# Tile-wise waits for re-opened pools, bank pairs in order of completion, and weights fetched two ahead in a three-part transformer kernel

## Chip, cores and metric

The kernel runs on one core of a Trainium2 chip. The metric is the device time of one execution in microseconds, as the median of several runs; before the change it is 1088.41 us.

## What is computed

```python
def reference(**kwargs):
    attn_out = _attn_ref(**attn_kwargs)     # 4 batches, 12 heads, 448 tokens, head size 64
    B, H, S, D = attn_out.shape
    x = np.ascontiguousarray(attn_out.transpose(0, 2, 1, 3)).reshape(B * S, H * D)   # 1792 x 768
    x = _moe_ref(x=x, **moe_kwargs)
    return _moe2_ref(x=x, **moe2_kwargs)

def _attn_ref(q, k, v, cap):
    scores = scale * np.matmul(q, k.transpose(0, 1, 3, 2))
    scores = cap * np.tanh(scores / cap)
...
def _moe_ref(x, w_in, w_out):
    h = x @ w_in                            # 768 -> 2048
    g = h - np.tanh(h)
    return (g @ w_out).astype(np.float32)   # 2048 -> 768

def _moe2_ref(x, w_in, w_out):
    h = x @ w_in
    g = h * (1.0 / (1.0 + np.exp(-1.702 * h)))
    return (g @ w_out).astype(np.float32)
```

The two weight pairs arrive as float64; activations are float32.

## The kernel before

Every large product is done with three matmuls on fp32r operands: an operand is split into a high part (`hi_act`, a cast on ScalarE, L75) and a low part (`lo_dve`, a subtraction on VectorE, L87), and high x high, low x high and high x low are summed in PSUM. The float64 weights are read as pairs of 32-bit words and turned to float32 on chip (L192 on ScalarE, L201 and L207 on VectorE), then split into `wh` and `wl`, of which three buffers each exist.

The 1792 tokens go through in two parts: part 0 of 768 tokens, whose first up projection is partly run inside attention, and part 1 of 1024. A part is worked in two halves called spans, of 384 or 512 columns. The stages on the matmul engine (PE), with the time at which the profiled execution does them:

- 0 to 300 us: attention, and `gemm_in(0)` of part 0 (L848);
- 300 to 402 us: `gemm_out` (L878), the first down projection of part 0. It makes six 128-row outputs `e` in two "halves" of three. A half runs over eight weight chunks `j`; in each chunk the three sums of span 0 are added to, then the three of span 1, six matmuls each. After the last chunk `x_out` casts each finished sum on ScalarE and makes its low part on VectorE: these are the next layer's `x`;
- 402 to 504 us: `gemm_in(1)`, its result through a sigmoid GELU (L785);
- 504 to 592 us: `gemm_rows_seven` (L1073), the second down projection with seven block products (`ps_o`) in place of eight; its results leave through copies at L1109;
- 592 to 724 us: `gemm_in(0)` of part 1, its result through `g_cubic` (L749 on ScalarE, L750 on VectorE, then four more steps); 16 blocks `f`;
- 724 to 843 us `gemm_out_seven` (L920), to 960 us `gemm_in_seven` (L1002), to the end `gemm_rows_seven` again.

PSUM has eight banks. Two belong to `ps_s` for the whole program. The other six are used either as three pairs (pool `pair`) or as six single banks (pool `m`): `open_banks` closes one pool and opens the other on the same banks between stages. Likewise `swap_pools`, `open_plain` and `end_of_x` open SBUF pools in mid-program on bytes that released pools held. A pool opened in this way makes each of its new tiles wait for all users of the pools that held its bytes, whichever tile those used.

ScalarE, VectorE and the DMA queue of SyncE (SP) each work through their instructions in program order. A scheduler fixes that order from priorities; `tc.high_priority(offset=150)` moves what stands under it earlier.

Weights that are already float32 come as a stream: `w_next` hands out chunk `i`, `prepare` splits it, `fetch` starts the transfer from DRAM. Raw chunks land in the two buffers of `wr_p` (shown as `whole`); in `gemm_rows_seven` a third buffer, `spare`, is used for every third one. The chunks named `kept` are already split and land in `wh` and `wl` directly.

Of the kernel before, what the change touches and what calls it, by code (L numbers as in the profile page):

```python
# [9 lines left out]
F32 = mybir.dt.float32  # L10
# [24 lines left out]
def attention_moe_moe(ctx, tc, q, k, v, cap, w_in1, w_out1, w_in2, w_out2, out):  # L35
# [3 lines left out]
    P = 128  # L39
# [6 lines left out]
    KF = DF // P  # L46
# [11 lines left out]
    def pool(name, bufs, **kw):  # L58
        return ctx.enter_context(tc.tile_pool(name=name, bufs=bufs, **kw))
# [7 lines left out]
    ps_s = pool("ps_s", 2, space=bass.MemoryType.PSUM)  # L67
# [6 lines left out]
    def hi_act(dst, src):  # L74
        pin(nc.scalar.copy(out=dst, in_=src))  # L75
# [10 lines left out]
    def lo_dve(dst, src, hi):  # L86
        pin(nc.vector.tensor_tensor(out=dst, in0=src, in1=hi.bitcast(F32), op=ALU.subtract))  # L87
# [14 lines left out]
    xh, xl = list(xs_h[0]), list(xs_l[0])  # L102
# [25 lines left out]
    end_of_x = ExitStack()  # L128
# [5 lines left out]
    def open_second_x():  # L134
        some.pop("stack").close()
        end_of_x.close()
        n = TOKENS[1]
        rest = 2 * KM * (n - TOKENS[0])
        p = end_of_x.enter_context(tc.tile_pool(name="end_of_x", bufs=1, side="right"))
        t = p.tile([P, rest], F32R, name="x_end")  # L140
        slots = [x_big[:, a:a + n] for a in range(0, x_big.shape[1], n)] + [t[:, a:a + n] for a in range(0, rest, n)]
        xs_h.append(slots[:KM])
        xs_l.append(slots[KM:])
        open_temps()
# [20 lines left out]
    dbls, raws, whl, some = {}, {}, {}, {}  # L165
    n_raw, third = [0], []
# [110 lines left out]
    def fetch(i):  # L277
        if R0 <= i < len(stream) and not 0 <= i - R0 - len(rows_stream) < A0 and i not in whole:
            src, n, _ = stream[i]
            parts = src if isinstance(src, list) else [src]  # L280
            n_raw[0] += 1
            whole[i] = third[0] if third and n_raw[0] % 3 == 0 else wr_p.tile([P, WC], F32, tag="wr", name="whole")
            whole[i] = whole[i][:, :n]
            w = n // len(parts)
            for m, part in enumerate(parts):
                nc.sync.dma_start(out=whole[i][:, m * w:(m + 1) * w], in_=part)

    def prepare(upto):
        while n_ready[0] <= min(upto, len(stream) - 1):
            i = n_ready[0]  # L290
            if i < R0 and i not in early:
                with ExitStack() as behind:
                    if i < 2 * LEAD + 2:
                        for ins in marks:
                            behind.enter_context(tc.issue_after(ins))
                    convert(i)
                if i == R0 - 1:
                    fetch(R0)
                continue
            whl[i] = tuple(wh_p.tile([P, WC], F32R, tag=tag, name=tag) for tag in ("wh", "wl"))  # L300
            src, n, _ = stream[i]
            fetch(i)
            if i in whole:
                x = whole.pop(i)
                h, l = (t[:, :n] for t in whl[i])
                with tc.high_priority(offset=150):
                    hi_act(h, x)
                    lo_dve(l, x, h)
            else:
                for m, t in enumerate(whl[i]):  # L310
                    nc.sync.dma_start(out=t[:, :n].bitcast(F32), in_=src[:, m])
            fetch(i + 1)
            n_ready[0] += 1

    def w_next():
# [368 lines left out]
    def swap_pools(**kinds):  # L684
        if "stack" in some:
            some.pop("stack").close()
        some.clear()
        some["stack"] = ExitStack()
        for name, bufs in kinds.items():
            some[name] = some["stack"].enter_context(tc.tile_pool(name=f"some_{name}", bufs=bufs, side="right"))  # L690

    def open_wide():
        swap_pools(far=1, v=1)
# [7 lines left out]
    def open_banks(pairs):  # L701
        ps_stack.close()
        psum.clear()
        name, bufs = ("pair", 3) if pairs else ("m", 6)
        psum[name] = ps_stack.enter_context(tc.tile_pool(name=f"ps_{name}", bufs=bufs, space=bass.MemoryType.PSUM))
        if not pairs:
            for _ in range(2):
                one_bank("pass_over")

    def pair_of_banks(name):  # L710
        return psum["pair"].tile([P, 2, 512], F32, tag="pair", name=name)

    def one_bank(name):
        return psum["m"].tile([P, 512], F32, tag="m", name=name)
# [77 lines left out]

    def open_plain():
        g_stack.close()
        p = pool("g_plain", 1)
        gr.extend(p.tile([P, NT], F32, name=f"gr{i}") for i in range(KF))
        spare.append(p.tile([P, WC], F32, name="spare"))
        ring.extend([p.tile([P, HT], F32R, name=f"r{m}{i}") for m in "hl"] for i in range(KH))
# [32 lines left out]
    def gemm_in(layer):  # L831
        for f in f_order[layer]:
            i, (wh, wl) = w_next()
            pair = [] if "pair" not in psum else pair_of_banks("ps_h")
            for span, (a0, a1) in enumerate(SPANS[now[0]]):
                a = slice(a0, a1)
                if isinstance(pair, list):
                    pair.append(ps_s.tile([P, 512], F32, tag="s", name="ps_h")[:, :a1 - a0])
                    ps = pair[-1]
                else:  # L840
                    ps = pair[:, span, :a1 - a0]
                if layer:
                    seq = [(w, x, kk) for w, x in ((wh, xh), (wl, xh), (wh, xl)) for kk in range(KM)]
                else:
                    seq = [p for kk in range(KM) for p in ((wh, xh, kk), (wh, xl, kk))]
                    seq += [(wl, xh, kk) for kk in range(KM)]
                for m, (w, x, kk) in enumerate(seq):
                    pin(nc.tensor.matmul(ps, w[:, kk, :], x[kk][:, a], start=(m == 0), stop=(m == len(seq) - 1)))  # L848
                    if m == 0:
                        (beside_it if a0 else ahead)(i)  # L850
                    if m == LATE_AT:
                        run_late()
                    if m < len(seq) - 1:
                        yield
                if a0:
                    (g_cubic, g_gate)[layer](f, pair)
                yield

    def x_out(e, a, x):
        hi_act(xh[e][:, a], x)  # L860
        lo_dve(xl[e][:, a], x, xh[e][:, a])

    def gemm_out():
        for half in range(2):
            tiles = [pair_of_banks("ps_y") for _ in range(2 + half)]
            ps = [[t[:, span] for t in tiles] for span in range(2)]
            if not half:
                for bank in ps:
                    bank.append(ps_s.tile([P, 512], F32, tag="s", name="ps_y"))
            for j in range(KF // 2):  # L870
                i, (wh, wl) = w_next()
                for (a0, a1), bank in zip(SPANS[0], ps):
                    for e in range(3):
                        c = slice(e * P, (e + 1) * P)
                        seq = [p for kk in range(2) for p in ((wh, gh, kk), (wh, gl, kk))]
                        seq += [(wl, gh, kk) for kk in range(2)]
                        for m, (w, x, kk) in enumerate(seq):
                            nc.tensor.matmul(  # L878
                                bank[e][:, :a1 - a0], w[:, kk, c], x[2 * j + kk][:, a0:a1],
                                start=(j == 0 and m == 0), stop=(j == KF // 2 - 1 and m == len(seq) - 1),  # L880
                            )
                        if e == 0 and j < KF // 2 - 1:
                            (beside_it if a0 else ahead)(i)
                        if a0 == 0 and e == 1:
                            run_late()
                            if half == j == 0:
                                swap_pools(wd=1, wr=1)
                                dbl_dma()
                    if j == KF // 2 - 1:
                        for e in range(3):  # L890
                            x_out(3 * half + e, slice(a0, a1), bank[e][:, :a1 - a0])
                if j == KF // 2 - 1:
                    ahead(i)

# [138 lines left out]
    def gemm_rows_seven():  # L1033
# [10 lines left out]
            open_second_x()  # L1044
        room = [t[:, a:a + HW] for t in four_of_pairs() for a in (0, HW)]
        p1, u2 = room[:nt], room[nt:2 * nt]
        third.append(spare[0])
        todo = [divmod(n, KM) for n in range(2 * KM)] if another else []
        loaded = []
        step = 0  # L1050
# [2 lines left out]
        for p, name in enumerate(SEVEN_B):  # L1053
# [36 lines left out]
            for n in range(nt):  # L1090
# [9 lines left out]
                    rows_out(1, n, ps[n], u2[n])  # L1100
                elif not end:
                    rows_out(0, nt + n, ps[n])
        third.clear()

    def rows_out(half, n, ps, plus=None, two=False):
        tag = ("q", "v", "t", "far")[n % 4] if now[0] else ("q", "v", "q")[n % 3]
# [117 lines left out]
```

## Time and profile before

| | us |
|---|---|
| runs | 1084.84, 1088.41, 1088.77 |
| median | 1088.41 |
| the profiled execution, its own time | 1082.34 |
| its span in the trace | 1080.5 |
| PE busy in the span | 1065.3 (99%) |
| VectorE (DVE) busy | 806.2 (75%) |
| ScalarE (ACT) busy | 640.9 (59%) |

The span is what the trace covers, from the first instruction to the last; the profiled execution's own time is 1.84 us more. "Busy" of PE counts matmuls as the profile models them: a matmul's modelled end lies later than the start of the next, so a busy PE has no gap, but can still be slow if its clock is granted only in part (PEclk).

### The profile page before, as it was taken

The page shows a single profiled execution, that of the slowest core. Times are in us where ns is not written, and L with a number is a line of the kernel's source. Part 1 is how long each engine was busy: PE and PEld are TensorE (multiplying, and loading weights), DVE is VectorE, ACT ScalarE, POOL GpSimd, SP SyncE. Part 2 cuts the span into 40 slices and gives each one's busy share as a digit, 9 for nine tenths or more (in the row PEclk, how much of TensorE's full clock was granted, in tenths as well). Part 3 has the DMA queues.
Part 4 walks back from the last instruction along what each step waited for, and adds up shares of the span by engine and source line. Part 5 has one row for each costly group of instructions (what it writes and reads, how often), then busy time and mean ns, then how long its engine had stood idle before and what let it go on. Part 6 is the DMA issues. An engine that isn't in the chain of part 4 may idle for free.

```text
span 1080.5 us, 15254 instructions
## 1 busy us (share of the span) xinstructions
PE 1065.3 (99%) x5555; PEld 873.3 (81%) x5555; DVE 806.2 (75%) x1062; ACT 640.9 (59%) x850; POOL 54.5 (5%) x56
## 2 busy tenths in 40 slices
PE   9999999999999999999999999999999999999998
PEld 3333333799998999999999888878888788899998
DVE  4678989799986668676984688787968755489562
ACT  6898898699854344444673555564545443355552
POOL 0012343200000000000000000000000000000000
PEclk9999999999999999999999999999999999999999
DMA  6776678699769989886667885312332233334342
GB/s 143 184 215 197 183 198 252 201 311 300 252 216 365 346 288 358 307 296 194 199 203 227 298 283 176 107 48 75 101 102 82 94 91 98 93 100 129 98 126 73
DMA packets 146979, 205.58 MB, mean 190 GB/s; under 512 B 57628, under 2 KB 97112, under 8 KB 146904
## 3 DMA queue, kind: packets, MB, share of 16 engines
q1 hardware_dynamic: 145480, 203.82, 59.7%
q8 instruction: 44, 0.72, 0.3%
q10 hardware_dynamic: 1424, 0.79, 0.2%
q14 instruction: 31, 0.25, 0.1%
HBM read 145.49 MB, written 59.07 MB: 189 GB/s over the span
## 4 chain that ended last, share of the span: by engine, by line
PE 85%; DVE 5%; DMA 4%; ACT 3%; issue 2%; SPq 0%; DVEq 0%; ACTq 0%
PE ps_h L848 23%; PE ps_o L1073 19%; PE ps_y L920 11%; PE ps_h L1002 10%; PE ps_pv L530 7%; PE ps_sc L489 5%; PE ps_y L878 5%; DMA wd<-in_moe_w_out_dram 3%; PE ps_qk L468 1%; PE ps_tl L499 1%; PE ps_r L537 1%; DVE g_t L761 1%; DVE g_q L763 1%; PE ps_qk L477 1%; DVE g_q L764 1%
## 5 line engine op out<-in xcount | busy, mean ns | idle before, releaser
L848 PE MATMUL ps_h<-x,wh 128*128 128x384 f32 (+1 forms) x1056 | 224.9, 349 | 0.6 <-ACT o L1109 0.6
L848 PEld LDWEIGHTS ps_h<-x,wh 128*128 128x128 f32 x1056 | 188.0, 188 | 12.9 <-ACT o L1109 0.9
L75 ACT CAST rh<-gr 128x512 fp32r<-128x512 f32 (+1 forms) x173 | 101.2, 586 | 130.9 <-PE ps_o L1073 68.7
L87 DVE TENSOR_TENSOR rl<-gr,rh 128x512 fp32r<-128x512 f32 (+1 forms) x173 | 111.2, 644 | 55.1 <-ACT rh L75 53.2
L1073 PE MATMUL ps_o<-wh,rh 128*128 128x384 f32 x392 | 131.1, 334 | 1.6 <-ACT gr L785 1.6
L1073 PE MATMUL ps_o<-wh,rl 128*128 128x384 f32 x392 | 131.0, 334 | 0.0
L1073 PE MATMUL ps_o<-wl,rh 128*128 128x384 f32 x392 | 130.9, 334 | 0.0
L75 ACT CAST wh<-whole 128x768 fp32r<-128x768 f32 (+1 forms) x99 | 79.9, 808 | 79.9 <-PE ps_h L1002 42.5
L848 PE MATMUL ps_h<-x,wl 128*128 128x384 f32 (+1 forms) x576 | 126.5, 354 | 0.0
L848 PEld LDWEIGHTS ps_h<-x,wl 128*128 128x128 f32 x576 | 103.5, 188 | 9.7 <-issue 1.4
L87 DVE TENSOR_TENSOR wl<-whole,wh 128x768 fp32r<-128x768 f32 (+1 forms) x99 | 91.3, 924 | 23.4 <-ACT wh L75 20.6
L508 ACT ACTIVATE t<-ps_sc,tsc 128x896 f32<-128x896 f32 x72 | 69.8, 1004 | 22.4 <-PE ps_sc L489 22.4
L1073 PEld LDWEIGHTS ps_o<-wh,rh 128*128 128x128 f32 x392 | 73.6, 188 | 2.0 <-ACT gr L785 2.0
L1073 PEld LDWEIGHTS ps_o<-wl,rh 128*128 128x128 f32 x392 | 73.6, 188 | 0.0
L1073 PEld LDWEIGHTS ps_o<-wh,rl 128*128 128x128 f32 x392 | 73.6, 188 | 0.0
L510 ACT ACTIVATE t<-t,cpos 128x896 f32<-128x896 f32 x72 | 72.3, 1040 | 0.4
L489 PE MATMUL ps_sc<-qk 64*128 64x448 f32 x288 | 67.9, 570 | 0.8 <-ACT qk L75 0.6
L920 PE MATMUL ps_y<-rh,wh 128*128 128x512 f32 x168 | 66.1, 394 | 2.4 <-DVE g_far L750 2.4
L878 PE MATMUL ps_y<-gh,wh 128*128 128x384 f32 x192 | 64.2, 335 | 2.5 <-DVE x L87 2.5
L920 PE MATMUL ps_y<-rl,wh 128*128 128x512 f32 x168 | 66.1, 393 | 0.0
L920 PE MATMUL ps_y<-rh,wl 128*128 128x512 f32 x168 | 65.9, 392 | 0.0
L530 PE MATMUL ps_pv<-t,rv 128*64 128x448 f32 x288 | 63.7, 548 | 1.4 <-ACT t L508 1.4
(133 smaller groups left out, 1881.7 us busy)
## 6 DMA issues: line engine op xcount, KB each, us to landing
wd<-in_moe_w_in_dram SPq DMA_DIRECT2D x64, 384.0 KB
wd<-in_moe_w_out_dram SPq DMA_DIRECT2D x32, 768.0 KB
whole<-single SPq DMA_DIRECT2D x37, 384.0 KB
single<-wr SPq DMA_DIRECT2D x32, 384.0 KB
whole<-s SPq DMA_DIRECT2D x32, 384.0 KB
wh<-kept SPq DMA_DIRECT2D x25, 384.0 KB
wl<-kept SPq DMA_DIRECT2D x25, 384.0 KB
whole<-t SPq DMA_DIRECT2D x21, 384.0 KB
```

The costliest lines, as they stand in the source:

```text
L75: pin(nc.scalar.copy(out=dst, in_=src))
L87: pin(nc.vector.tensor_tensor(out=dst, in0=src, in1=hi.bitcast(F32), op=ALU.subtract))
L468: pin(nc.tensor.transpose(ps[:, c * CP:(c + 1) * CP], raw[g][:CP, 0, c * P:(c + 1) * P], ident[:CP, :CP]))
L489: pin(nc.tensor.matmul(ps[:, j, :S], qk[a, kc], qk[a, :S], start=True, stop=True))
L508: pin(nc.scalar.activation(out=t, in_=ps[:, :, :S], func=AF.Tanh, scale=tsc))
L510: ins = pin(nc.scalar.activation(out=tt[g, c], in_=tt[g, c], func=AF.Exp, scale=cpos))
L530: pin(nc.tensor.matmul(ps[a, :S], w, t[:, j], start=(c == 0), stop=(c == KC - 1)))
L848: pin(nc.tensor.matmul(ps, w[:, kk, :], x[kk][:, a], start=(m == 0), stop=(m == len(seq) - 1)))
L878: nc.tensor.matmul(bank[e][:, :a1 - a0], w[:, kk, c], x[2 * j + kk][:, a0:a1], start=(j == 0 and m == 0), stop=(j == KF // 2 - 1 and m == ...
L920: nc.tensor.matmul(ps[e], w[:, kk, c], x, start=(name == head and k == 0 and m == 0), stop=(k == KH - 1 and m == 2), skip_group_check=True,)
L1002: nc.tensor.matmul(ps, w, x, start=(name == head and m == 0), stop=(m == len(seq) - 1), skip_group_check=True,)
L1073: nc.tensor.matmul(ps[n], x[:, t], w[:, kk, :], start=(first and k == 0 and m == 0), stop=(k == KH - 1 and m == 2), skip_group_check=True,)
```

## The change

Pools that are opened in mid-program get `reuse_waits="tile"`: a new tile waits for those users only that touched its own bytes, or for PSUM its own bank. The two banks that were taken and thrown away at each change to single banks (`pass_over`) are gone. Block `f = 0` of the up projection at part 1 takes two `ps_s` banks in place of a pair. In `gemm_out` the bank pairs are handed out in the order in which the sums end, and a pair's two sums are cast and split together as soon as both have ended. `fetch` runs two chunks ahead where the third buffer exists, and the third buffer stays in use after `gemm_rows_seven`.

```diff
@@ open_second_x, swap_pools, open_plain: the same argument at each
-        p = end_of_x.enter_context(tc.tile_pool(name="end_of_x", bufs=1, side="right"))
+        p = end_of_x.enter_context(tc.tile_pool(name="end_of_x", bufs=1, side="right", reuse_waits="tile"))
...
@@ prepare
-            fetch(i + 1)
+            for n in range(1, 2 + len(third)):
+                fetch(i + n)
@@ open_banks
-        psum[name] = ps_stack.enter_context(tc.tile_pool(name=f"ps_{name}", bufs=bufs, space=bass.MemoryType.PSUM))
-        if not pairs:
-            for _ in range(2):
-                one_bank("pass_over")
+        psum[name] = ps_stack.enter_context(tc.tile_pool(
+            name=f"ps_{name}", bufs=bufs, space=bass.MemoryType.PSUM, reuse_waits="tile"
+        ))
@@ gemm_in
-            pair = [] if "pair" not in psum else pair_of_banks("ps_h")
+            pair = [] if "pair" not in psum or now[0] and f == 0 else pair_of_banks("ps_h")
@@ gemm_out
+        def x_of_banks(ready):
+            with tc.high_priority(offset=150):
+                for e, a, x in ready:
+                    hi_act(xh[e][:, a], x)
+                for e, a, x in ready:
+                    lo_dve(xl[e][:, a], x, xh[e][:, a])
+            ready.clear()
+
         for half in range(2):
-            tiles = [pair_of_banks("ps_y") for _ in range(2 + half)]
-            ps = [[t[:, span] for t in tiles] for span in range(2)]
+            banks = [t[:, n] for t in [pair_of_banks("ps_y") for _ in range(2 + half)] for n in range(2)]
             if not half:
-                for bank in ps:
-                    bank.append(ps_s.tile([P, 512], F32, tag="s", name="ps_y"))
+                banks += [ps_s.tile([P, 512], F32, tag="s", name="ps_y") for _ in range(2)]
+            ps = [banks[:3], banks[3:]]
+            ready = []
...
-                    if j == KF // 2 - 1:
-                        for e in range(3):
-                            x_out(3 * half + e, slice(a0, a1), bank[e][:, :a1 - a0])
+                        if j == KF // 2 - 1:
+                            ready.append((3 * half + e, slice(a0, a1), bank[e][:, :a1 - a0]))
+                            if len(ready) == 2 or a0 and e and not half:
+                                x_of_banks(ready)
@@ gemm_rows_seven
-        third.append(spare[0])
+        third[:] = spare
...
-        third.clear()
```

PE's rows at the last chunk of `gemm_out`'s first half, before; `ps_y_3064` and `ps_y_3065` are bank pairs, `ps_y_3066` and `ps_y_3067` single `ps_s` banks, `ps_y_3504` the first pair of the second half, and every sum has six matmuls, of which one or two stand here:

```order
L878 MATMUL ps_y_3064<-gh15_2071,wl_3353 128x384
L878 MATMUL ps_y_3065<-gh14_2070,wh_3352 128x384
L878 MATMUL ps_y_3066<-gh14_2070,wh_3352 128x384
L878 MATMUL ps_y_3064<-gh14_2070,wh_3352 128x384 [waits DVE_49]
L878 MATMUL ps_y_3065<-gh14_2070,wh_3352 128x384 [waits DVE_49]
L878 MATMUL ps_y_3067<-gh14_2070,wh_3352 128x384
L878 MATMUL ps_y_3504<-gh0_2056,wh_3405 128x384 [waits Activation_49]
```

And with the change, the same place, the six sums in order:

```order
L886 MATMUL ps_y_3064<-gh15_2071,wl_3353 128x384
L886 MATMUL ps_y_3064<-gh14_2070,wh_3352 128x384
L886 MATMUL ps_y_3065<-gh14_2070,wh_3352 128x384
L886 MATMUL ps_y_3066<-gh14_2070,wh_3352 128x384
L886 MATMUL ps_y_3067<-gh14_2070,wh_3352 128x384
L886 MATMUL ps_y_3504<-gh0_2056,wh_3405 128x384 [waits Activation_49]
```

Before, the fourth sum (the first of span 1) lies in the pair of the first and carries a wait for VectorE; now the two sums of a pair follow each other, and no sum of this chunk waits for VectorE before the second half begins.

VectorE's rows at that place, before (`group` is a sum of raw weights, `x` the low parts, `wl`, `wd` and `wr` weights in conversion):

```order
L347 TENSOR_TENSOR group<-group 128x768 x2
L87 TENSOR_TENSOR wl<-wr,wh 128x768
L201 TENSOR_SCALAR wd<-wd 128x768
L87 TENSOR_TENSOR x<-ps_y,x 128x384 x2
L207 SCALAR_TENSOR_TENSOR wr<-wr,wd 128x768
L87 TENSOR_TENSOR x<-ps_y,x 128x384 x2
L347 TENSOR_TENSOR group<-group 128x768
```

And with the change (L348 is L347 of before):

```order
L348 TENSOR_TENSOR group<-group 128x768 x2
L87 TENSOR_TENSOR wl<-wr,wh 128x768
L201 TENSOR_SCALAR wd<-wd 128x768
L348 TENSOR_TENSOR group<-group 128x768
L87 TENSOR_TENSOR x<-ps_y,x 128x384 x2
L207 SCALAR_TENSOR_TENSOR wr<-wr,wd 128x768
L87 TENSOR_TENSOR x<-ps_y,x 128x384 x3
```

One `group` addition that stood behind four low parts now stands ahead of the first two. ScalarE has the casts of the pairs at the place where it had the casts of the three sums of span 0, behind the same L192.

SP's rows in the up projection of part 1, before (`s_0` to `s_3` are sums of weight blocks that are stored, `single` and `kept` weights in DRAM):

```order
L286 DMA whole<-single_155 128x768
L311 DMA wh<-kept_142 128x768
L311 DMA wl<-kept_142 128x768
L376 DMA s_0_203<-pair 128x768
L376 DMA s_0_211<-pair 128x768
L376 DMA s_0_207<-pair 128x768
L286 DMA whole<-single_156 128x768
L376 DMA s_0_215<-pair 128x768
L311 DMA wh<-kept_143 128x768
```

And with the change (L377 is L376 of before):

```order
L286 DMA whole<-single_156 128x768
L311 DMA wh<-kept_142 128x768
L311 DMA wl<-kept_142 128x768
L377 DMA s_0_203<-pair 128x768
L377 DMA s_0_211<-pair 128x768
L286 DMA whole<-single_157 128x768
L377 DMA s_0_207<-pair 128x768
L311 DMA wh<-kept_143 128x768
```

The first raw chunk, `single_155`, has gone into the third buffer at the end of part 0's rows, and the loads of this stretch are those of the two chunks behind it; PE's order differs from that of before in the banks alone.

## Rows read from the trace of the kernel before

**Rows 1.** The page: span, and busy time by engine.

```profile
span 1080.5 us, 15254 instructions
PE 1065.3 (99%) x5555; PEld 873.3 (81%) x5555; DVE 806.2 (75%) x1062; ACT 640.9 (59%) x850; POOL 54.5 (5%) x56
```

**Rows 2.** Waits of PE after 200 us: in total, times, longest.

```profile
PE ps_y L878 <- DVE x L87: 2.5, 1, 2.5
PE ps_y L920 <- DVE g_far L750: 2.4, 1, 2.4
PE ps_o L1073 <- ACT gr L785: 1.6, 1, 1.6
PE ps_h L1002 <- ACT wh L75: 0.7, 1, 0.7
```

**Rows 3.** Windows of two stages: length, PE, PEld, DVE, ACT, POOL, clock, DMA, GB/s.

```profile
348.80:402.10 53.30, 53.30 (x307) 53.30 (x308) 34.46 (x50) 21.86 (x30) 0.00 (x0) 1.00 0.90 320
591.80:724.20 132.40, 132.39 (x576) 108.11 (x576) 104.63 (x100) 71.09 (x71) 0.00 (x0) 1.00 0.58 187
```

**Rows 4.** Timeline, 345 to 352 us: start, duration, instruction, idle before it and releaser.

```profile
345.81 0.51 PE L878 MATMUL ps_y<-gh,wl 128*128 128x384 f32 x2
...
345.87 0.91 ACT L192 ACTIVATE wr<-wd 128x768 f32<-128x768 f32 x1 [1.09 <-DMA wd<-in_moe_w_out_dram]
346.69 1.22 ACT L75 CAST x<-ps_y 128x384 fp32r<-128x384 f32 x3
...
348.17 1.02 DVE L87 TENSOR_TENSOR x<-ps_y,x 128x384 fp32r<-128x384 f32 x2
348.77 0.44 PE L878 MATMUL ps_y<-gh,wh 128*128 128x384 f32 x1 [2.45 <-DVE x L87]
...
351.12 0.95 DVE L347 TENSOR_TENSOR group<-group 128x768 f32<-128x768 f32 x1
```

**Rows 5.** Timeline at 906 us.

```profile
906.53 0.50 PE L1002 MATMUL ps_h<-x,wl 128*128 128x512 f32 x1
906.87 0.62 PE L1002 MATMUL ps_h<-x,wh 128*128 128x512 f32 x2
```

**Rows 6.** Timeline at 496 and 503 us.

```profile
496.49 0.81 ACT L785 ACTIVATE gr<-ps_h 128x768 f32<-128x768 f32 x1
...
503.58 0.45 PE L1073 MATMUL ps_o<-wh,rh 128*128 128x384 f32 x1 [1.63 <-ACT gr L785]
```

**Rows 7.** Timeline at 591 us.

```profile
591.81 1.45 PE L848 MATMUL ps_h<-x,wh 128*128 128x512 f32 x5 [0.57 <-ACT o L1109]
```

**Rows 8.** Timeline at 717 and 726 us.

```profile
717.05 1.23 DVE L750 TENSOR_TENSOR g_far<-ps_h,g_t 128x1024 f32<-128x1024 f32 x1
...
726.58 0.68 PE L920 MATMUL ps_y<-rh,wh 128*128 128x512 f32 x1 [2.37 <-DVE g_far L750]
```

**Rows 9.** Windows from that matmul on; the granted clock is third from the end.

```profile
726.50:727.00 0.50, 0.42 (x1) 0.39 (x2) 0.40 (x2) 0.50 (x1) 0.00 (x0) 0.73 0.72 227
727.00:730.00 3.00, 3.00 (x8) 2.30 (x7) 2.79 (x3) 1.58 (x2) 0.00 (x0) 0.50 0.21 84
730.00:732.00 2.00, 2.00 (x10) 1.63 (x9) 1.30 (x2) 0.11 (x1) 0.00 (x0) 0.96 0.00 0
```

**Rows 10.** Waits of ScalarE, whole span: in total, times, longest.

```profile
ACT rh L75 <- PE ps_o L1073: 68.7, 78, 1.8
...
ACT wh L75 <- PE ps_y L878: 18.7, 8, 5.0
...
ACT wh L75 <- DMA whole<-s: 13.7, 8, 3.2
```

**Rows 11.** Timeline of VectorE and SP's queue, 582 to 725 us.

```profile
582.79 0.96 DVE L87 TENSOR_TENSOR wl<-whole,wh 128x768 fp32r<-128x768 f32 x1 [1.72 <-ACT wh L75]
...
604.16 0.45 SPq L286 DMA_DIRECT2D whole<-single  x1
...
708.79 8.57 SPq L286 DMA_DIRECT2D whole<-single  x2
```

More of the change, by code (lines that the diff above doesn't have):

```diff
@@ L689, in swap_pools @@
         for name, bufs in kinds.items():
-            some[name] = some["stack"].enter_context(tc.tile_pool(name=f"some_{name}", bufs=bufs, side="right"))
+            some[name] = some["stack"].enter_context(tc.tile_pool(name=f"some_{name}", bufs=bufs, side="right", reuse_waits="tile"))
     def open_wide():
@@ L794, in open_plain @@
         g_stack.close()
-        p = pool("g_plain", 1)
+        p = pool("g_plain", 1, reuse_waits="tile")
         gr.extend(p.tile([P, NT], F32, name=f"gr{i}") for i in range(KF))
```

## The prediction

> **What bounds the kernel now.** I read the busy times first. PE is busy for 1065.3 of the 1080.5 us of the span [rows 1], so all its idle time together is 15.2 us. No edit here takes a matmul away or makes one shorter, so this is nearly all there is to win, and the question is which part of it hangs on waits that the change removes. The list of PE's waits names them: after 200 us there are two of about 2.4 us, one of 1.6, and small ones [rows 2]. The stage windows give PE's pace where nothing holds it: 53.30 us for 307 matmuls of 384 columns, or 0.174 us each, and 132.40 us for 576 of 512 columns, or 0.230 us each [rows 3]. Then I read the timeline at each wait, to see what released PE and what that had waited for itself.
>
> **How a wait is priced.** The idle time in a bracket starts at the modelled end of the last matmul, and that lies later than the moment when the next could have started. At 345.81 two matmuls last 0.51 us: one step of 0.17 and a modelled length of 0.34 [rows 4]. So the idle bracket misses 0.34 - 0.17, about 0.16 us. Behind a wait the first step is also longer: 0.34 us in place of 0.23 at 906.53 [rows 5], which is 0.11 more. A wait that vanishes gives back its bracket plus 0.27 us.
>
> **First sums of part 0, 348.77 us.** PE starts the fourth sum of the last chunk after 2.45 us of idling, released by the low part of x [rows 4]. That sum lies in the pair of the first sum, so it waits until the first has been cast and subtracted. The chain behind it starts at a DMA: ScalarE waited 1.09 us for weights `wd`, did L192 at 345.87 and only then the casts at 346.69; VectorE's lows followed at 348.17 [rows 4]. With the change, sums four to six need no bank that is waited for. PE goes on at 345.81 + 2 x 0.174 = 346.16. The first pair is needed again by the third sum of the second half, 18 + 12 = 30 matmuls later, at 346.16 + 30 x 0.174 = 351.4. On VectorE one `group` addition of 0.95 us now stands ahead of the lows, so the first two end at about 348.17 + 0.95 + 1.02 = 350.1 [rows 4]. That leaves 1.2 us. The gain is 2.45 + 0.27 = 2.72 us. Its bounds are 0, if the lows come 1.2 + 2.7 = 3.9 us later than I place them, and 2.72.
>
> **Change to single banks, 503.58 us.** The first matmul of `ps_o` waited 1.63 us for the last GELU, although that one read the last pair. With waits by bank it needs the GELUs before it, of which the latest started at 496.49 and took 0.81 us [rows 6], so it ended at 497.30, 4.4 us before PE gets there at about 501.7. Gain 1.63 + 0.27 = 1.90 us; not below 0, since no new work stands ahead of it.
>
> **Change to pairs, 591.81 us.** PE waited 0.57 us for the copies of `o` [rows 7]. Block 0 takes `ps_s` banks now, and does not wait for them; block 1 comes 36 x 0.230 = 8.3 us later. Gain 0.57 + 0.27 = 0.84 us, and 0 if the kept weights, which come by DMA, are only just there.
>
> **Change to single banks at part 1, 726.58 us.** PE waited 2.37 us for `g_far` of block 15. Now the first three banks are those of blocks 13 and 14, and the subtraction of block 14 started at 717.05 and took 1.23 us [rows 8], so it ended 6 us before PE arrives at about 724.1. Block 15's banks are wanted only by the second product, 4 chunks x 18 = 72 matmuls or 16 us on. The idle is worth 2.37 + 0.16 = 2.53 us. Behind it the clock falls: it is 0.73 for half a microsecond, 0.50 (the 1.2 GHz level) for 3.0 us, and 0.96 for 2 us [rows 9]. Against full clock that loses 0.42 x 0.27 + 3.0 x 0.50 + 2.0 x 0.04 = 1.7 us, the slow first step included. If the idling is the cause, this goes with it: 4.23 us together, and 2.53 if it is not.
>
> Does the idle time cause that? The rows are of two minds: 2.37 us of idling was followed by the low level [rows 8, 9], 2.45 us at 348.77 was not, since the stage behind it reads 1.00 [rows 4, 3]. So idling of this size may lower the clock in some executions and not in others. Had the timed runs seen no such drop, they would win 9.9 - 1.7 = 8.2 us by the sum below; had the waits at 348.77 and 503.58 cost them 1.7 us each as well, 9.9 + 3.4 = 13.3 us. My sum takes what this execution shows. The Trainium skill (TensorE: Matmul & The Clock Gate, "Part 1: The HAM clock gate") says that half clock is the default, that activity lifts it, and that the moment of a change varies from run to run. By that rule a drop behind one stall and none behind its like are both to be expected, and the gain lies anywhere between the two figures; the trace agrees so far, with one drop behind two stalls of 2.4 us.
>
> **Weights two ahead.** ScalarE waits 13.7 us in 8 pieces for raw chunks [rows 10], but PE feels only two of them, with a step 0.11 us longer each, of which 906.53 is one [rows 5]. Gain 0.2 us, bounds 0 and 0.5. The third buffer is freed by the same event as the second was (the split of the chunk three before instead of two), so SP's queue waits for nothing later than before.
>
> **Costed at nothing.** Block 0's tanh and subtraction in two pieces add two short instructions; ScalarE is busy for 71.09 and VectorE for 104.63 of that stage's 132.40 us [rows 3], which covers them; uncovered they cost under 0.5 us. The SBUF pools with waits by tile are opened where no wait of PE stands in the list. The 0.7 us on `wh` at L1002 [rows 2] hangs on in-order work inside that stage and stays.
>
> **Sum.** 2.72 + 1.90 + 0.84 + 4.23 + 0.2 = 9.9 us. The profiled execution took 1082.34 us, 1.84 more than its span and 6.1 less than the median of the runs. 9.9 of 1082.34 is 0.91%; taken off 1088.41 that gives **1078.5 us**.
>
> **Rivals.**
>
> *The first wait only moves (1081.2 us).* If L192's weights land later than here, casts and lows slip behind the third sum of the second half, and PE stands there instead. For it speaks that ScalarE and VectorE keep their order and the DMA share is 0.90 there [rows 3]; against it the 1.2 us of room. Moved in full it takes 2.72 off the gain: 7.2 us.
>
> *The clock acts otherwise (1080.2 or 1075.1 us).* The gain is the 8.2 or the 13.3 us worked out above. For it speaks the spread of the runs, 3.9 us, above the profiled execution; against the upper gain, that the rows show one drop only.
>
> *The gain is handed back (about 1083 to 1088 us).* PE is ahead by 2.7 us from 346 on and by 4.6 from 504, and may run into weights that come at DMA's pace. If these two gains are lost at the next weights, 5.3 us stay, and the time is 1083.1, a change of 0.49%. Against it: in `gemm_out` the split of weights waits for PE to free a buffer (18.7 us in 8 waits), and in the rows stage the casts wait for PE 78 times [rows 10], so PE is not fed at the last moment; it has no gap at all in 53.30 us behind the first wait [rows 3].
>
> *SP's queue is blocked (slower, about 1160 us).* In part 1 a second `whole` load stands in SP's order between two stores, ahead of the kept weights of block 4. Had its buffer a reader left, those weights would stand behind it. The buffer's last reader before was the split at 582.79, and the load goes out from 604.16 on [rows 11]: 20 us of room. Were it instead the next split, which frees a buffer for the load at 708.79 [rows 11], block 4, due at 591.8 + 4 x 8.3 = 625, would come 84 us late. It decides against the change from about 10 us of delay behind block 4's due time, which uses up the gain.
>
> **Chances.** The forecast has 0.58, the moved wait 0.10, the clock 0.10 (two thirds of it on the smaller gain), the gain handed back 0.18, the blocked queue and its like 0.04. A measurement of this kernel can tell about 0.5%, or 5.4 us, from no change, so faster means below 1083.0. All but the last two cases lie there, as does a small part of the handed-back gain: faster 0.78, same 0.18, slower 0.04. The range goes from 1074.0, the larger gain with 1 us to spare, to 1085.0, which takes in the moved wait, the smaller clock gain and the better half of the handed-back case.
>
> **What would show it.** PE's list of waits after 200 us should hold L1002's 0.7 us and nothing over 1 us; the first `ps_o` and the first `ps_y` of part 1 should start 0.2 us after the matmul before them; the windows behind the latter should read a clock of 1.00; PE's idle time in the span should be 15.2 - 2.45 - 1.63 - 0.57 - 2.37 = 8.2 us. The lows of the first pair should end about 1 us before the third sum of the second half. I am wrong if a wait of over 1 us stands at that third sum, if the clock still falls near 720 us, or if PE's idle time falls by 7 us and the span does not.

## The result and the profile after

The changed kernel takes 1073.13 us (median of six runs, 1071.57 to 1076.10), against 1084.33 us for the kernel before, whose three runs shown above became six (1081.69 to 1088.77). The ratio is 0.9891, with a 95% interval of 0.9864 to 0.9918: 1.1% faster. The forecast was 1078.5 us in a range of 1074.0 to 1085.0, so the time lies 0.9 us below the range. The direction was right, and the forecast gain of 0.91% lies inside the interval; the forecast time does not fit, since it was taken off a median that more runs moved.

The page of the profiled execution (its own time is 1071.57 us), span and busy times:

```profile
span 1069.8 us, 15251 instructions
PE 1061.2 (99%) x5555; PEld 871.9 (82%) x5555; DVE 804.0 (75%) x1063; ACT 641.1 (60%) x851; POOL 54.4 (5%) x56
```

PE is idle for 8.6 us in place of 15.2 [rows 1]; 8.2 were forecast. The list of PE's waits after 200 us, which had five entries (the four of [rows 2] and the 0.57 us of [rows 7]), has one:

```profile
PE ps_h L1011 <- ACT wh L75: 0.7, 1, 0.7
```

The timeline at the four places of [rows 4, 6, 7, 8], in the same order:

```profile
349.45 1.01 DVE L87 TENSOR_TENSOR x<-ps_y,x 128x384 fp32r<-128x384 f32 x2
350.74 0.33 PE L886 MATMUL ps_y<-gh,wh 128*128 128x384 f32 x1
...
497.38 1.20 PE L848 MATMUL ps_h<-x,wh 128*128 128x384 f32 x6
498.42 0.33 PE L1082 MATMUL ps_o<-wh,rh 128*128 128x384 f32 x1
...
585.78 1.78 PE L848 MATMUL ps_h<-x,wh 128*128 128x512 f32 x7
...
717.88 0.39 PE L929 MATMUL ps_y<-rh,wh 128*128 128x512 f32 x1
```

None of these matmuls has a bracket: the first `ps_o` starts one step (0.17 us) after the last of the six matmuls of `ps_h` ahead of it. One place is closer than forecast. The third sum of the second half starts at 350.74, and the low parts of the first pair end at 349.45 + 1.01 = 350.46, 0.28 us earlier; the forecast left 1.2 us there.

The windows that answer to [rows 9] read full clock:

```profile
717.50:718.00 0.50, 0.50 (x4) 0.42 (x3) 0.15 (x1) 0.04 (x1) 0.00 (x0) 1.00 0.00 0
718.00:721.00 3.00, 3.00 (x15) 2.49 (x14) 2.72 (x3) 2.86 (x3) 0.00 (x0) 1.00 0.28 53
```

Between the two traces the span falls by 1080.5 - 1069.8 = 10.7 us. The sum named 9.9 of it. Another 0.6 us comes from the start, where the first eleven matmuls take less time, before and with the change:

```profile
1.19 4.88 PE L1167 MATMUL wps<-wz 128*128 128x512 bf16 x11 [1.19 <-DVE cub_u L1174]
1.19 3.97 PE L1175 MATMUL wps<-wz 128*128 128x512 bf16 x11 [1.19 <-DVE cub_u L1182]
```

They last 3.97 us in place of 4.88: their step halves, from 0.43 to 0.22 us, within the eleven, and behind them in the trace before. No edit is at work there.

Both traces hold the same 5555 matmuls in the same order of forms, so PE's lead over the trace before can be read off matmul by matmul. It is 0.62 us ahead of the first wait, 3.37 behind it, 5.30 behind the first `ps_o`, 6.17 in block 1 of part 1, 10.41 behind the first `ps_y` of part 1 and 10.69 at the end. The steps are 2.75, 1.93, 0.87, 4.24 and 0.28 us, where the sum has 2.72, 1.90, 0.84, 4.23 and 0.2. So between these two traces the sum holds, term by term. It is the step from one trace to the median that failed, and the experiments show why.

### The profile page after: what moved, and what is told of

It reads as the page before. It is cut to its first block, busy times and chain, and to the rows that moved or that the text cites. A ratio compares the mean times of both kernels' runs of the same rounds, so it can differ in the third digit from the quotient of the medians.

```text
span 1069.8 us, 15251 instructions
## 1 busy us (share of the span) xinstructions
PE 1061.2 (99%) x5555; PEld 871.9 (82%) x5555; DVE 804.0 (75%) x1063; ACT 641.1 (60%) x851; POOL 54.4 (5%) x56
## 4 chain that ended last, share of the span: by engine, by line
PE 96%; ACT 1%; DVE 1%; SPq 1%; DMA 1%; issue 0%; DVEq 0%; ACTq 0%
PE ps_h L848 31%; PE ps_o L1082 19%; PE ps_y L929 11%; PE ps_h L1011 10%; PE ps_y L886 9%; PE ps_pv L531 7%; PE ps_sc L490 5%; PE ps_tl L500 1%; PE ps_qk L469 1%; PE ps_r L538 1%; PE ps_qk L478 1%; PE ps_qk L479 0%; ACT t L509 0%; DMA capr<-in_cap_dram 0%; SPq L429 0%
## 5 line engine op out<-in xcount | busy, mean ns | idle before, releaser
L75 ACT CAST wh<-whole 128x768 fp32r<-128x768 f32 (+1 forms) x78 | 63.2, 810 | 49.0 <-PE ps_h L1011 32.1
L87 DVE TENSOR_TENSOR wl<-whole,wh 128x768 fp32r<-128x768 f32 (+1 forms) x78 | 72.0, 924 | 9.9 <-ACT wh L75 8.0
L192 ACT ACTIVATE wr<-wd 128x768 f32<-128x768 f32 x48 | 44.2, 920 | 44.8 <-DMA wd<-in_moe_w_out_dram 19.7
```

The source lines that it names most:

```text
L192: pin(nc.scalar.activation(out=raws[i][:, :width[i]], in_=dbls[i][:, :, 1].bitcast(F32), func=AF.Prelu, scale=2.0 ** -112, alpha=2.0 ** 32))
```

## The experiments

Theory 1 is that of the prediction: the gain is the sum of four waits of fixed size. Theory 2: a part comes from elsewhere, such as weights that come earlier. Theory 3 came out of the first four runs: the first wait and the clock behind the waits differ from run to run, so that one trace does not give their size.

Differences from the changed kernel's 1073.13 us are between sets of runs taken at different times, and the kernel before had medians from 1084.8 to 1087.0 us beside these sets. So a difference of less than about 2 us is not read from the times alone.

**Waits by pool for the PSUM banks.**

```diff
-        psum[name] = ps_stack.enter_context(tc.tile_pool(..., reuse_waits="tile"))
+        psum[name] = ps_stack.enter_context(tc.tile_pool(...))
```

> The changed kernel, but pools of PSUM banks wait for all users of the pool before them again. Theory 1 (the gain is the sum of the waits that vanished): the waits at the first ps_o of part 0 and at the first ps_y of part 1 come back, 1.63 + 0.27 = 1.9 us and 2.53 us, and where the clock falls behind the second 1.7 us more; 4.4 to 6.1 us over the changed kernel's 1073.1, so 1077.5 to 1079.2 us. Block 0 keeps its ps_s banks, so nothing comes back at 587 us. Theory 2 (a part of the gain stems from elsewhere, such as weights that come earlier): less than 4 us comes back. On the clock: if idling of 2.4 us lowers it each time, the stage behind the first ps_y reads 1.7 us of lost clock; if the drop is a matter of chance, it may read none, and the one at the first ps_o may read some.

Measured: 1078.64 us (ratio to before 0.9940, interval 0.9925 to 0.9955), 5.5 us more than the changed kernel. Three of its five waits of PE after 190 us, and a window behind the first:

```profile
PE ps_y L927 <- DVE g_far L748: 2.4, 1, 2.4
PE ps_o L1080 <- ACT gr L783: 1.6, 1, 1.6
...
PE ps_y L884 <- DVE x L87: 0.5, 1, 0.5
```

```profile
725.00:727.00 2.00, 2.00 (x9) 1.66 (x10) 1.88 (x2) 1.97 (x2) 0.00 (x0) 1.00 0.47 164
```

Both waits came back with the size that they had before, as theory 1 says, and none at block 0. But after the same 2.37 us of idling the clock stays at 1.00, where it fell in [rows 9]. And 0.5 us of the first wait stands at the third sum of the second half.

**The old order of the sums.** `gemm_out` is that of the kernel before.

```diff
-            ps = [banks[:3], banks[3:]]
+            ps = [[t[:, span] for t in tiles] for span in range(2)]
...
-                                x_of_banks(ready)
+                            x_out(3 * half + e, slice(a0, a1), bank[e][:, :a1 - a0])
```

> The changed kernel with gemm_out as it was (sums of one pair lie in both spans, three casts after each span). Theory 1: the wait of 2.45 us at the fourth sum of the first half's last chunk comes back, worth 2.7 us: 1075.8 us. The clock behind it reads 1.00 as in the kernel before, or 1.7 us are lost if chance decides. Theory 2: under 1.5 us comes back, since the weights behind it would be waited for anyway.

Measured: 1079.64 us (0.9949, 0.9935 to 0.9964), 6.5 us more than the changed kernel and not 2.7. The timeline, and a window of the clock behind it:

```profile
345.38 0.93 ACT L192 ACTIVATE wr<-wd 128x768 f32<-128x768 f32 x1 [1.94 <-DMA wd<-in_moe_w_out_dram]
...
347.23 1.95 DVE L348 TENSOR_TENSOR group<-group 128x768 f32<-128x768 f32 x2
...
350.42 1.02 DVE L87 TENSOR_TENSOR x<-ps_y,x 128x384 fp32r<-128x384 f32 x2
...
351.03 0.69 PE L878 MATMUL ps_y<-gh,wh 128*128 128x384 f32 x1 [4.11 <-DVE x L87]
```

```profile
351.00:356.00 5.00, 4.97 (x16) 4.97 (x17) 3.41 (x6) 1.77 (x3) 0.00 (x0) 0.52 1.01 389
```

The wait is 4.11 us here and not 2.45, and behind it the clock is at its lower level for nearly 5 us, which costs 5.00 x 0.48 = 2.4 us: 4.11 + 0.16 + 2.4 = 6.7 us for what I had priced at 2.72.

**One fetch ahead.**

```diff
-            for n in range(1, 2 + len(third)):
-                fetch(i + n)
+            fetch(i + 1)
...
+        third.clear()
```

> The changed kernel with one fetch ahead and the third buffer given up after part 0's rows, as before. Theory 1: two steps of 0.11 us come back at about 896 and 925 us; 1073.3 us, not to be told from the changed kernel. Theory 2: 1 to 2 us come back, with waits of PE on weights in the windows from 720 to 950 us.

Measured: 1073.25 us, the changed kernel's time within 0.1 us. One step is late again, by 0.15 us of idling:

```profile
925.92 0.50 PE L1010 MATMUL ps_h<-x,wl 128*128 128x512 f32 x1 [0.15 <-DVE wl L87]
```

As theory 1 says: the fetch ahead is worth a few tenths of a microsecond at most. The moved wait shows too, with 0.2 us.

**The waits by bank alone, in the kernel before.**

```diff
-        psum[name] = ps_stack.enter_context(tc.tile_pool(...))
-        if not pairs: ... one_bank("pass_over")
+        psum[name] = ps_stack.enter_context(tc.tile_pool(..., reuse_waits="tile"))
```

> The kernel before with the waits by bank alone (and without the two banks thrown away). Theory 1: the waits of 1.63 and 2.37 us go, and most of the 0.57 at block 0, since its pair waits for the copies out of its own two banks only; 2.45 us at 348 us stays. Gain 1.9 + 2.5 to 4.2 + 0 to 0.8 us of the 1084.3: 1077.4 to 1079.9 us. Theory 2: a gain under 4 us.

Measured: 1082.46 us (0.9984, 0.9972 to 0.9996), so a gain of 2.4 us and not 4.4 to 6.9. Its longest waits of PE:

```profile
PE ps_y L877 <- DVE x L87: 4.1, 1, 4.1
PE ps_y L919 <- DVE g_far L749: 2.5, 1, 2.5
```

The waits of 1.63 and 0.57 us are gone, worth 2.7 us together, and that at the first `ps_y` of part 1 is not. So waits by bank alone do not do what I had put down to them there.

**Block 0 in a pair again, in the changed kernel.**

```diff
-            pair = [] if "pair" not in psum or now[0] and f == 0 else pair_of_banks("ps_h")
+            pair = [] if "pair" not in psum else pair_of_banks("ps_h")
```

> The changed kernel with block 0 of part 1 in a bank pair again; waits by bank stay. Reading of the kernel with waits by bank alone, which kept 2.46 us at the first ps_y of part 1 and had none at block 0: waits by bank alone suffice at 587 us, and block 0's place matters at 720 us, since 16 blocks in rotation over three pairs put block 15 into the first pair, whose banks the first ps_y takes, and 15 blocks put it into the last. So the wait of 2.4 us comes back at about 720 us (2.5 us, or 4.2 where the clock falls), none at 587: 1075.6 to 1077.3 us. My prediction's reading (block 0 in ps_s banks saves the wait at 587 us, waits by bank the one at 720): a wait of 0.57 us at 587 us, none at 720, 1074.0 us.

Measured: 1077.48 us, 4.3 more than the changed kernel (0.9919 of before, 0.9898 to 0.9940). The kernel before stood at 1087.01 us beside it; by the two ratios, 0.9919 and 0.9891, it is 3.0 us more. The list of waits has none at block 0, but:

```profile
PE ps_y L929 <- DVE g_far L750: 2.5, 1, 2.5
PE ps_h L1011 <- ACT wh L75: 0.7, 1, 0.7
PE ps_y L886 <- DVE x L87: 0.4, 1, 0.4
```

With 16 blocks in three pairs the last block has the first pair, whose banks the first `ps_y` takes; with 15 it has the last. The wait at part 1 goes only if both edits are made: waits by bank, and block 0 elsewhere.

**The kernel before, once more.**

> The kernel before, unchanged, profiled once more. Theory 1 (the first wait has a fixed size): 2.4 to 2.5 us at the fourth sum of the first half's last chunk. Theory 3 (its size is that of the way from the weights' landing to the low part, about 2.6 to 2.9 us from the start of L192, so it moves with a landing that differs from run to run): anything from 2.4 to about 5 us, PE's release 2.6 to 2.9 us behind the start of that L192, and the clock lowered or not behind it.

Measured: 1087.24 us, where the first profiled execution took 1082.34, from the same program. Its timeline, and two windows behind its two long waits:

```profile
346.04 0.95 ACT L192 ACTIVATE wr<-wd 128x768 f32<-128x768 f32 x1 [1.92 <-DMA wd<-in_moe_w_out_dram]
...
347.90 1.95 DVE L347 TENSOR_TENSOR group<-group 128x768 f32<-128x768 f32 x2
...
351.10 1.02 DVE L87 TENSOR_TENSOR x<-ps_y,x 128x384 fp32r<-128x384 f32 x2
...
351.71 0.47 PE L878 MATMUL ps_y<-gh,wh 128*128 128x384 f32 x1 [3.66 <-DVE x L87]
```

```profile
352.00:355.00 3.00, 3.00 (x11) 3.00 (x11) 2.12 (x5) 1.18 (x2) 0.00 (x0) 0.50 0.97 379
...
731.50:734.50 3.00, 3.00 (x9) 2.28 (x9) 2.79 (x3) 1.55 (x2) 0.00 (x0) 0.54 0.24 97
```

The first wait is 1.2 us longer, and the clock falls behind both. The waits of 1.63, 0.57 and 2.37 us are the same to the hundredth. So those have a fixed size, and the first has not.

Matmul by matmul, the first wait and the clock behind it make 2.7 us of the 1085.2 - 1080.5 = 4.7 us between the two spans. Another 1.3 us comes with a wait inside attention, ahead of 200 us, that neither the first trace nor that of the changed kernel has:

```profile
196.37 0.97 PE L530 MATMUL ps_pv<-t,rv 128*64 128x448 f32 x4 [1.20 <-ACT t L508]
```

It stands in seven of the fifteen traces, of kernels with the old and with the new order of the sums. So it is no part of the gain, but it is a part of the difference between executions; what brings it is not shown.

In the first trace the same L192, the one before that of [rows 4], is this row:

```profile
343.14 0.92 ACT L192 ACTIVATE wr<-wd 128x768 f32<-128x768 f32 x1 [1.89 <-DMA wd<-in_moe_w_out_dram]
```

From its start to PE's release it is 348.77 - 343.14 = 5.63 us there, 5.67 here and 5.65 in the kernel with the old order of sums, with idle times of 2.45, 3.66 and 4.11 us. The kernel with waits by bank alone has 5.65 us as well (344.55 to 350.20), with 4.12 us of idling. The way is fixed; its start is a landing of weights, which keeps no step with PE. On this way VectorE works without a gap: L207, two additions, `wl`, `wd`, the low part.

In the changed kernel the same landing is what used up the room at the third sum:

```profile
343.55 0.92 ACT L192 ACTIVATE wr<-wd 128x768 f32<-128x768 f32 x1 [1.91 <-DMA wd<-in_moe_w_out_dram]
```

This L192 starts 0.41 us later than in the trace before, while PE was 0.62 us earlier: 1.03 us together, and the room shrank from 1.2 to 0.28.

**One more transfer of 768 KB.** In both kernels, ahead of the load that the later L192 waits for:

```diff
+            if i == 27:
+                with tc.issue_after(last_load[0]):
+                    nc.sync.dma_start(out=more_load..., in_=src...)   # nothing reads it
```

> The kernel before with one more transfer of 768 KB from the weights to DRAM, which nothing reads, put on SP's queue right ahead of the load that the L192 ahead of the casts waits for. Theory 1 (fixed size): no change beyond 0.3 us. Theory 3 (the landing sets it): the wait at the fourth sum grows by about the time of one such transfer, 2 to 3 us, and the kernel takes 2 to 4 us more than before where the clock falls too.

> The changed kernel with the same additional transfer. Theory 1: no change. Theory 3: casts and lows of the first pair come 2 to 3 us later, which the 30 matmuls up to the third sum of the second half cover but for 1 to 2 us: a wait of that size there and 1 to 2 us more than 1073.1, so less than what the kernel before loses by the same transfer.

Measured: 1084.03 us (0.9992, 0.9974 to 1.0009) in the kernel before, and 1073.91 us in the changed one, with 0.28 us of idling at the third sum. The 2 to 4 us that theory 3 expected in the kernel before did not come. But this did not part the theories cleanly, since the scheduler moved the first casts ahead of that L192 in both. With this order of the casts, that L192 (L202 here) started only at 348.24, and PE was released at 348.78 all the same:

```profile
348.24 0.90 ACT L202 ACTIVATE wr<-wd 128x768 f32<-128x768 f32 x1 [1.80 <-DMA wd<-in_moe_w_out_dram]
...
348.78 0.44 PE L888 MATMUL ps_y<-gh,wh 128*128 128x384 f32 x1 [2.85 <-DVE x L87]
```

For the order of the kernel before, its own trace answers. The three casts take 1.22 us from 346.69 on [rows 4], so the first is done about a microsecond before VectorE comes to the low parts at 348.17. VectorE comes to them without idling, straight from this row:

```profile
347.70 0.56 DVE L201 TENSOR_SCALAR wd<-wd 128x768 uint32<-128x768 uint16 x1
```

So what ended last there was VectorE's queue, not the later landing, on which I had hung the chain.

**The additions later, and both queues later,** in the kernel before:

```diff
+        with ExitStack() as behind:            # ahead_of_side
+            for ins in behind_x:               # the second low part
+                behind.enter_context(tc.issue_after(ins))
...
+            for ins in behind_cast if i in (27, 28) else ():   # convert: L192 behind the second cast
+                behind.enter_context(tc.issue_after(ins))
```

> The kernel before with the additions of group (L347) queued on VectorE behind the first two low parts, and nothing else. Theory 3 in its second form (the way to the first wait runs through VectorE's own queue: earlier L192, L207, two group additions, wl, wd, then the low part, 5.6 to 5.7 us from the start of the earlier L192 in every trace): without the additions the casts behind the later L192 end last, so the wait at the fourth sum is 1.0 to 1.2 us shorter than in the kernel before, between 1.3 and 3 us from run to run, and the clock falls less often; 1 to 3 us less than before. First form (the later L192 and the casts alone set it): the wait keeps its 2.4 to 4.1 us.

> The kernel before with both queued behind: the group additions on VectorE behind the first two low parts, and the later L192 on ScalarE behind the first two casts. Theory 3: the fourth sum needs no landing of the weights any more, and its wait of 2.45 to 4.1 us goes, with the clock's fall behind it; the other waits (1.6, 0.6, 2.4 us) stay. 1085 less 4 to 6 us: 1079 to 1081 us. If the place of the sums in the bank pairs is what matters and not the queues, nothing changes.

The first has the upper part alone. Measured: 1084.12 us (0.9991, 0.9976 to 1.0005), no change, and a wait of 3.07 us. Its timeline (L196 is L192 of before, L211 is L207):

```profile
346.67 0.94 ACT L196 ACTIVATE wr<-wd 128x768 f32<-128x768 f32 x1 [1.29 <-DMA wd<-in_moe_w_out_dram]
...
347.63 0.96 DVE L211 SCALAR_TENSOR_TENSOR wr<-wr,wd 128x768 uint32<-128x768 uint32 x1 [0.41 <-ACT wr L196]
348.51 1.48 DVE L91 TENSOR_TENSOR x<-ps_y,x 128x384 fp32r<-128x384 f32 x3
349.11 0.69 PE L887 MATMUL ps_y<-gh,wh 128*128 128x384 f32 x1 [3.07 <-DVE x L91]
```

With the additions gone from the way, VectorE has its next L207 ahead of the low parts, and that one waits for the later landing: the expectation failed. The second kernel, with both queues behind: 1081.68 us (0.9971, 0.9959 to 0.9983), 3.6 us less than before, a little under the 4 to 6 expected.

```profile
345.49 0.95 ACT L196 ACTIVATE wr<-wd 128x768 f32<-128x768 f32 x1 [1.89 <-DMA wd<-in_moe_w_out_dram]
...
348.72 1.01 DVE L91 TENSOR_TENSOR x<-ps_y,x 128x384 fp32r<-128x384 f32 x2
...
349.32 0.44 PE L891 MATMUL ps_y<-gh,wh 128*128 128x384 f32 x1 [1.86 <-DVE x L91]
```

The way from the earlier L192 is 349.32 - 345.49 = 3.83 us, shorter than 5.65 by 1.82, and two additions take 1.86 from step to step. The wait did not go, as expected it would, but is 1.86 us with a late landing, and the clock stays up behind it. So in these traces the size of the first wait is set by the landing of the earlier weights plus what VectorE does in order behind it.

**The same two orders in the changed kernel.**

> The changed kernel with the same two orders. Theory 3: the remainder of the wait that shows up at the third sum of the second half when weights land late (0.2 to 0.5 us of idling in four traces of kernels with the new order) goes. 0 to 0.8 us less than the changed kernel, so 1072.3 to 1073.1: not to be told from it by the time, only by the list of waits. If the weights that are put behind come late instead, a wait on wh or wl of L886 appears.

Measured: 1072.65 us (median of six, 1071.95 to 1077.07), not to be told from 1073.13. PE's list has no wait at the third sum. No version that I ran beats the changed kernel by more than its runs differ.

**PE's order in `gemm_in_seven`.**

```diff
+                    if j < 2:
+                        tc.keep_in_program_order(ins)
```

> The changed kernel with PE's matmuls of the first two blocks of gemm_in_seven kept in program order. In the changed kernel the first matmul of the next block was put ahead of the last products of block 0 and waits 0.73 us for its weights, whose buffer is only then released; in program order its weights have about 4 us longer. If that is the cause, the wait of 0.73 us and its first step go, 0.9 to 1.0 us, and the two short ones ahead of it stay: 1072.2 us. If another wait takes its place (the low parts of last_t), nothing is won.

Measured: 1075.49 us, 2.4 more than the changed kernel; by the ratio to before (0.9910, 0.9896 to 0.9925) the intervals of the two overlap. The 0.73 us went, and another wait took its place:

```profile
842.07 0.50 PE L1011 MATMUL ps_h<-rh,wh 128*128 128x512 f32 x1 [2.48 <-DVE part L348]
```

The scheduler's order had hidden this wait for a sum on VectorE behind other products.

**Waits by pool for the SBUF pools.**

```diff
-            ... tc.tile_pool(name=f"some_{name}", bufs=bufs, side="right", reuse_waits="tile"))
+            ... tc.tile_pool(name=f"some_{name}", bufs=bufs, side="right"))
```

> The changed kernel with waits by pool again for the SBUF pools (end_of_x, some_*, g_plain); PSUM's pools keep waits by bank. As costed, nothing: 1073.1 us, and no new wait of PE. If the SBUF pools had a part in the gain, waits of PE appear at 200 to 210, 296 or 405 us.

Measured: 1073.59 us, and after 200 us PE's list holds the 0.7 us at L1011 alone, as in the changed kernel: these edits are worth nothing that can be measured.

## Why the prediction was right in kind and too small

Of the 1078.5 - 1073.1 = 5.4 us between forecast and measurement, 4.0 lie in the median that the gain was taken off, and 1.4 in the size of the gain, 0.91% against 1.09%, which is within the noise of the comparison.

**Where the time comes from: right.** Nearly all of it comes from the four waits and the clock behind them, and the waits of 1.63, 0.57 and 2.37 us had just the price of the sum.

**The first wait, 2.72 us: mis-sized.** Between the two traces it gave 2.75 us, but that is the size of one execution. The step that failed is "ScalarE waited 1.09 us for weights `wd`, did L192 at 345.87 and only then the casts". The wait hangs on the landing one load earlier and on VectorE's queue behind it. I took the idle time of one execution for a constant; it was 2.45 us there and 3.66, 4.11 and 4.12 us in the three other traces that have the old order and no other edit at this place.

**The clock, 1.7 us: mis-sized.** The sum took one drop, "what this execution shows". In the 13 runs of the kernel before that were timed beside the first four experiments, the mean granted clock was 0.9966 (0.9968 in all 54 beside the experiments), which loses 0.0034 x 1085 = 3.7 us; in the six of the changed kernel it was 0.9993, or 0.7 us. The drops that went are worth 3.0 us on the mean, not 1.7. The larger gain that I worked out for the clock, 13.3 us, was weighed too low. Half of its ground held: the clock fell behind the first wait in three of the four traces just named. The other half did not: in six traces with 1.63 us of idling at the first `ps_o`, the clock never fell there.

An estimate with these sizes, 3.6 us for the first wait (the mean of the four traces) and 3.0 us for the clock, gives 9.9 + 1.1 + 1.3 = 12.3 us, against 11.2 between the medians.

**From the trace to the median: wrong.** This is the step that put the forecast outside. "6.1 less than the median of the runs" took 1088.41 from three runs, two of which lie above each of the 54 runs of that kernel that were timed beside the experiments (up to 1088.2); the medians of the later sets are 1084.8 to 1087.0. The profiled execution had a short first wait and one drop, so it lay low, and two of the three runs lay high. A gain read from the one and set against the other gave 1078.5. Set against 1084.33, the same 0.91% would have given 1074.5.

**Which edit does what: half wrong.** Block 0's place was credited with 591.81 us, where waits by bank suffice, and not with 726.58 us, where it is needed beside them. The sum is not touched, since both edits are made.

**Two ahead, SBUF pools: right**, with 0.1 us between medians (0.28 us between the two traces) and nothing.

**The rivals.** The moved wait happens in part: 0.2 to 0.5 us at the third sum in four of the other traces with the new order, since 0.28 us of room is less than the landings vary. The gain was not handed back, and SP's queue was not blocked: PE has no other wait.

## What to carry to other kernels

A wait whose chain begins at a landing may have no size of its own, as the first wait here had none: find the first link that keeps no step with the waiting engine, and read it in more than one execution before it goes into a sum. Set a gain that was read from one execution against that execution, and ask where it lies among the runs before it is set against their median. When a pool of banks is opened on another, look which tile the last user holds: waits by bank help only if the rotation leaves the first bank to an earlier one.

## What the runs showed of the hardware

I read the granted clock behind every wait of PE of half a microsecond or more at the places of [rows 4, 6 to 8], at the third sum, and, where PE's order was kept, in `gemm_in_seven`; ten traces have such waits. After idling of 0.5 to 1.9 us it never fell (13 times). After 2.37 to 2.48 us it fell 5 times in 10, at one and the same place too: it fell at the first `ps_y` of part 1 after 2.37 us in the kernel before, and did not after the same 2.37 us in the kernel with waits by pool. After 2.85 to 4.12 us it fell 5 times in 5. Behind the wait, with PE at work, the lower level lasted 3 to 5 us each time. In these traces the length of the idling alone does not tell whether 2.4 us of it lower the clock.

The rule that I cited from the Trainium skill (TensorE: Matmul & The Clock Gate, "Part 1: The HAM clock gate") is that the moment of a change varies from run to run. The first eleven matmuls agree with it: their step halves at different matmuls in the two traces. That a fall behind 2.4 us of idling comes in some executions and not in others, and what it costs on the mean, only the runs show.
